# Linear attention and feed-forward on one core: the denominators of split units transposed by VectorE straight from PSUM, fewer filling products, and a new order of the steady part

## The chip, the cores and the metric

The kernel runs on one core of a Trainium2 chip. The engines that matter are TensorE (PE: matmuls; PEld: its weight loads), VectorE (DVE), ScalarE (ACT), GpSimd (POOL) and the queue that issues transfers (SP). The metric is device time in microseconds (us), the median of three runs; lower is better.

## The reference, cut to what matters

```python
# attention: 8 batches x 8 heads, 576 tokens, head size 64, 128 features
phi(x)  = exp(h - max(h)) / sqrt(128),  h = x @ omega.T - sum(x*x)/2,  x scaled by 64 ** -0.25
q_p, k_p = phi(q), phi(k)
kv  = einsum('bhsm,bhsd->bhmd', k_p, v);  z = sum(k_p, axis=2)
num = einsum('bhsm,bhmd->bhsd', q_p, kv)
den = einsum('bhsm,bhm->bhs', q_p, z)[..., None] + 1e-06
attn = num / den
# feed-forward on x = attn with the heads side by side: 4608 tokens x 512
h = x @ w_in                      # 512 x 2048
out = gelu(h) @ w_out             # 2048 x 512, gelu with erf
```

The sum of squares and the factors common to numerator and denominator cancel and aren't computed; the 1e-06 is kept, scaled.

## The kernel before, in words

**Work.** Attention is done in 32 units of two heads each (four units to a batch). The first eight units are "plain": float32 products. The other 24 are "split": a float32 value is carried as a high and a low part, and products use the parts. The feed-forward takes the tokens in 13 blocks: block 0 of 128 tokens in float32 (lines 1176 and 1202), blocks 1 to 11 of 384 tokens and block 12 of 256, whose operands are split into two float16 parts. Of such a block `mm1` (L1181) makes 16 chunks of h with 12 products each, ScalarE applies gelu (L1189) and casts the high part (`g_high`, L1193), VectorE makes the low part (`g_low`, L1197), and `mm2` (L1205 to L1207) multiplies with the second weight.

**A unit's end.** For each half of a unit's tokens (288 columns for both heads), `num_plain` (L737) or `num` (L746) writes numerators and denominators into two PSUM tiles called `pn`, out of a ring `at` of three buffers that the attention's other products use too (in the first batch, other rings too). In a plain unit `rcp` (L763 to L766) lets VectorE transpose the denominator in 32x32 blocks from PSUM into `rt`, so that nine columns hold what is different, adds the small constant, takes the reciprocal of 128x9 values, and transposes these back, spread over 32 columns. In a split unit the numerator of one head lies beside the denominator of the same head in the other half of the partitions. There `den` (L757) is two ScalarE instructions that copy the two denominators of 64x288 from PSUM into one tile `dt` and add the constant; `rcp` then transposes `dt` (L768), takes the reciprocal (L769) and transposes back (L770). Last `div` (L803 in split units) multiplies into the tokens `xs` of the feed-forward, and the two `pn` tiles come free.

**Order.** Nothing is ordered at run time: each engine runs its own list. A planner at build time simulates all operations with a cost each (the second argument of `op`), and picks on each engine the ready operation with the earliest due time. Due times come from `STARTS` (blocks), `UDUE` (halves of units) and `OFF` (an offset for each kind of operation), with bonuses from `X`. The first operations, those named in the list `FIRST`, are put in the order of that list; it holds those of the first part, up to the middle of block 1. What comes after it follows the due times: the steady part, in which the products of blocks and those of attention units are interleaved.

**Filling products.** Where the planner finds TensorE without work, and its own clock is between `wk0` and `wk` microseconds, it emits `fill` (L381): four products of 128 columns of the identity matrix, whose result, in the unused columns 384 to 511 of the first buffer `hb`, is read by nobody.

**Queues.** SP issues all transfers in one order: `load_dup` (q and k of a split unit), `load_vst` (v of a batch), the weights' pieces, and the stores of finished rows. `x_low` (L894), `k_shift` (L920), `k_high` (through the helper at L352) and `w_round` (L453) are GpSimd's.

Of the kernel before, what the change touches and what calls it, by code (L numbers as in the profile page):

```python
# [14 lines left out]
AF = mybir.ActivationFunctionType  # L15
ALU = mybir.AluOpType
# [3 lines left out]
P = 128  # L20
T = 384
# [3 lines left out]
TOP = 13  # L25
TBS = (128,) + (384,) * 11 + (256,)

X = dict(fb=793.51, fbp=-272.45, fb0=327.13, fbb=-89.81, fbw=0.0, pm=0.088, tsw=1.28, wmaxp=0, plain=8, kvp=8, eb0=8, ttr=1,
         pair=0, amax=0, qm=1, xm=0, km=0, prelu=1, vs=1, rm=1, wk=100.0, wk0=5.0, nd=1, sr=0, pmx=0, m0=5)

STARTS = (526.64, 413.1, 498.14, -519.29, 750.73, 290.96, 409.8, 1471.02, 410.3, 561.38, 1804.53, 1092.9, 2449.47, 1437.07)
UDUE = (138.05, 1052.37, 451.76, -315.56, -8.29, -412.87, -648.85, -667.31, -702.59, -616.51, 659.91, -322.47, 26.1, 555.78,
# [4 lines left out]
OFF = dict(block_be=26.55, block_high=27.77, block_low=-66.27, block_out=-28.64, block_scales=3.6, block_spread=19.77,  # L39
           bound_b=-1.8, bound_c=-2.45, chain_a=-30.63, chain_b=-10.13, chain_c=-20.24, den=42.52, div=27.82, exp_tiles=19.68,  # L40
           exps=188.48, g_high=-4.72, g_low=-2.69, gelu=-0.61, k_high=-188.65, k_low=1.15, k_shift=6.34, kv=-46.75, kv_a=19.82,
           kv_b=26.2, kv_b2=28.0, kv_c=85.59, kv_d=-177.32, kv_split=-133.22, kvz_plain=-8.08, load_dup=-16.98, load_om=49.87,
           load_two=-48.56, load_v=-10.04, load_vraw=0.87, load_vst=9.94, mm1=-0.7, mm2=6.86, nothing=115.9, num=-9.4,
           num_plain=-14.95, p2=-1.38, pair=14.61, proj=20.5, proj_add=90.32, proj_lo=-1.05, proj_q=-2.91, q_back=-44.1,
           q_blocks=93.79, q_copy=3.3, q_high=-144.85, q_low=-2.94, q_max=87.36, q_max2=100.29, q_max3=-0.43, q_max4=12.08,
           q_max5=4.81, q_max6=-30.09, q_shift=-0.46, q_trans=-45.18, rcp=31.74, shared=-0.95, shift_tiles=7.84,
           split_om=35.99, store=-8.53, store_dma=-54.03, top=-1.35, v_a=53.83, v_b=-6.0, v_max=-0.96, v_scales=80.74,
           w_hi=58.87, w_high=6.68, w_lo=0.74, w_load=-11.85, w_low=3.77, w_rmax=11.16, w_round=-18.28, warm=5.19,
           wchain_a=35.94, wchain_b=91.67, wchain_c=-1.79, wchain_d=18.88, wchain_e=5.29, wchain_f=-87.86, x_high=-1.56,
           x_low=0.31, zeros=71.27)  # L50
FIRST = (1, 3, 0, 2, 6, 7, 8, 40, 4, 5, 42, 110, 76, 144, 41, 142, 10, 9, 151, 157, 44, 13, 43, 11, 14, 15, 47, 74, 16, 45, 17,
# [208 lines left out]
def favor_attention_ffn(ctx: ExitStack, tc: tile.TileContext, qT, kT, v, omT, w_in, w_out, out):  # L260
    nc = tc.nc
    B, H, D, S = qT.shape
    NJ = H // 2
# [4 lines left out]
    TB = TBS  # L268
    NBLK = len(TB)
    T0 = [sum(TB[:n]) for n in range(NBLK + 1)]  # L270
    assert T0[-1] == NTOK
    NF = F // P
    R2 = 2 * S
    NT = R2 // P
    NV = v.shape[3]
    HS = S // 2
    EPS = 1e-6 * M
# [5 lines left out]
    N32 = 1  # L283
# [12 lines left out]
    w32 = cp.tile([P, 2, NF, 512], I32, name="w32")  # L296
    w32f = w32.bitcast(F32)
    wi32 = w32f[:, 1].rearrange("p c (j w) -> p c j w", j=NJ)
# [19 lines left out]
    iz = ident.bitcast(BF16)  # L318
# [4 lines left out]
    op = PL.op  # L323
# [54 lines left out]

    def fill():
        for i in range(4):  # L380
            nc.tensor.matmul(hb[0][:, T:], iz[:, 0:P], iz[:, P:], start=True, stop=True)  # L381

    def load_om():
        for r in range(2):
# [209 lines left out]
    for b in range(B):  # L594
        for j in range(NJ):
            u = Obj()
# [162 lines left out]
    def rcp(u, half):  # L759
        rt, rc = G['rt', u, half], G['rc', u, half]  # L760
        rv = rt.rearrange("p (n c) -> p n c", c=32)
        if X['nd'] and not u.split:
            nc.vector.transpose(rt, G['pn', u, half, 1][:, 0:HS])  # L763
            nc.vector.tensor_scalar(rc, rv[:, :, 0], EPS, None, op0=ALU.add)
            nc.vector.reciprocal(rc, rc)
            nc.vector.transpose(rv, rc.unsqueeze(2).broadcast_to([P, HS // 32, 32]))  # L766
            return
        nc.vector.transpose(rt, G['dt', u, half])  # L768
        nc.vector.reciprocal(rc, rv[:, :, 0])  # L769
        nc.vector.transpose(rv, rc.unsqueeze(2).broadcast_to([P, HS // 32, 32]))  # L770
# [8 lines left out]
    def xs_place(n, j):  # L779
        if (n, j) not in xplace:  # L780
            if n < 2:
                xplace[n, j] = (xa[:, j, T0[n]:T0[n + 1]], ('xa', n, j))
            elif n == 2:
                xplace[n, j] = (None, ('xs', n, j))
            else:
                k = NKK + xk[0] % (NF - NKK)
                xk[0] += 1
                xplace[n, j] = (w32f[:, 1, k, 0:T], ('xw', k))
        return xplace[n, j]

    def xs(n, j):
        return xplace[n, j][0] if n != 2 else G['xs', n, j]
# [27 lines left out]
    def out_ops(u, half):  # L820
        ps, keys, new, pn = finish_unit(u, half)
        qs = (half,) if X['qm'] else (half, 2 + half)
        r = [('qh', u, g) for g in ((0, 1, 2) if not u.split else qs)]
        rr = [('kvz', u), ('qh', u)] if not u.split else [('kvh', u), ('kvl', u), ('qh', u)] + [('ql', u, g) for g in qs]
        ring = ANY if u.b == 0 else 'at'
        op('PE', 1.06 if not u.split else 0.8, num if u.split else num_plain, u, half, r=r + rr, w=keys,
           new=[(ring, k) for k in pn] + new)
        n = 0.5 if not u.split else 0.96
        if X['nd'] and not u.split:
            op('DVE', 1.06, rcp, u, half, r=pn, new=[('rt', ('rt', u, half)), ('rc', ('rc', u, half))])  # L830
        else:
            op('ACT', n, den, u, half, r=pn + ([('vsc', u.b)] if not u.kp else []), new=[('dt', ('dt', u, half))])
            op('DVE', 0.92, rcp, u, half, r=[('dt', u, half)], new=[('rt', ('rt', u, half)), ('rc', ('rc', u, half))])
        c = sum(0.15 + (c1 - c0) / 960 for _, c0, c1, _ in ps) * (2 if u.split else 1)
        op('DVE', c, div, u, half, due=(2, 2 * u.k + half, 0.0, 0.0), r=pn + [('rt', u, half)], w=keys + [k for _, k in new])
# [336 lines left out]
    def mm1(n, c, p):  # L1172
# [5 lines left out]
        for i in range(p * NJ, (p + 1) * NJ):  # L1178
            j, k = divmod(i, 3)
            w = (wih, wil, wih)[k][:, j, c * P:(c + 1) * P]  # L1180
            nc.tensor.matmul(h[:, 0:t], w, (G['xh', n, j], G['xh', n, j], G['xl', n, j])[k][:, 0:t], start=(i == 0), stop=(i == 3 * NJ - 1))  # L1181

    def gelu(n, c):
        t = TB[n]
        h = G['h', n, c][:, 0:t]
        if n < N32:
            nc.scalar.activation(G['g', n, c][:, 0:t], h, AF.Gelu)
        else:
            nc.scalar.activation(h, h, AF.Gelu, scale=G['bs', n][:, 2:3])  # L1189
# [37 lines left out]
    def when(n, c, add=0.0):  # L1227
        return (1, n + int(c >= NF), c % NF / NF, add)
# [16 lines left out]
    def ffn_first(n, c):  # L1245
        t = TB[n]
        k = 'F' if n >= N32 else 'F0'
        if n < N32:
            xr = [xs_place(n, j)[1] for j in range(NJ)]
            for p in range(3):  # L1250
                seq('m1', 'PE', (t * 4 / 2400 + .005) * (2, 1, 1)[p], mm1, n, c, p, r=[('w32', 1, c)] + xr, w=[('h', n, c)] if p else [],
                   new=[] if p else [('h', ('h', n, c))], due=when(n, c + p / 3), kind='P')
            op('ACT', 0.1 + t / 1000, gelu, n, c, r=[('h', n, c)], new=[('g', ('g', n, c))], tab='g', kind=k)
            return
        for p in range(3):
            xr = [(x, n, j) for j in sorted({i // 3 for i in range(p * NJ, (p + 1) * NJ)}) for x in ('xh', 'xl')]
            seq('m1', 'PE', 4 * (t / 2400 + .0025), mm1, n, c, p, r=[('wh', 1, c), ('w', 1, c)] + xr, w=[('h', n, c)] if p else [],
               new=[] if p else [('h', ('h', n, c))], due=when(n, c + p / 3), kind='P')
        op('ACT', 0.165 + t / 1000, gelu, n, c, r=[('bs', n)], w=[('h', n, c)], tab='g', kind=k)
        op('ACT', 0.15 + t / 900, g_high, n, c, r=[('bs', n), ('h', n, c)], new=[('gh', ('gh', n, c))], kind=k)  # L1260
        op('DVE', 0.09 + t / 850, g_low, n, c, r=[('bs', n), ('h', n, c), ('gh', n, c)], new=[('gl', ('gl', n, c))], kind=k)
# [135 lines left out]
```

## Time and profile before

| what | value |
|---|---|
| median of three runs | 976.9 us (976.35 to 977.07) |
| the profiled execution's own time | 975.53 us |
| its span in the trace | 973.8 us |
| PE busy | 963.4 us (99% of the span) |
| DVE, ACT, POOL busy | 715.4, 730.0, 350.4 us |
| granted TensorE clock | full speed |

Busy PE is counted from the start of a product to its modelled end; products overlap, so a product's mean duration in the tables (say 326 ns) is longer than the time from one start to the next. The pieces of the chain of work that ended last are free of that overlap. The span is the trace's; the time is the run's own clock around it, 1.7 us more here, and the profiled run lies 1.4 us below the median of the three.

### The profile page before, as it was taken

The numbers are of one execution on the slowest core, as the hardware profiler recorded it, in microseconds if no ns is written. First come the engines' busy times: TensorE is split into PE (matmuls) and PEld (weight loads), VectorE is DVE, ScalarE is ACT, GpSimd is POOL, SyncE is SP. The second block draws the span as 40 slices with busy tenths as digits, with TensorE's granted clock in tenths as the row PEclk, the third lists the DMA queues.
The fourth block names the chain that finished last, engine by engine and source line by source line (L and its number), as shares of the span: only waits on it lengthen the run. The fifth ranks groups of instructions, "written<-read, shape, count | busy, mean of one in ns | idle before, by whom it ended". The sixth has DMA issues, their size and how long they took to land.

```text
span 973.8 us, 18152 instructions
## 1 busy us (share of the span) xinstructions
PE 963.4 (99%) x6324; PEld 602.3 (62%) x6324; DVE 715.4 (73%) x1948; ACT 730.0 (75%) x1504; POOL 350.4 (36%) x560
## 2 busy tenths in 40 slices
PE   8999999999999999999999999999999999999998
PEld 7777665665566666666565665566656656555576
DVE  5899899977888889878797888777767778621111
ACT  6979897887689879787798878877776986643243
POOL 2444334742166264353255335245216522200000
PEclk9999999999999999999999999999999999999999
DMA  8756123321041041031221132022003200000000
GB/s 305 229 182 227 70 73 134 98 82 55 1 118 61 26 139 47 25 91 45 75 82 49 30 127 66 14 72 61 24 33 86 62 23 12 1 33 1 1 34 22
DMA packets 39083, 70.96 MB, mean 73 GB/s; under 512 B 5712, under 2 KB 14288, under 8 KB 38992
## 3 DMA queue, kind: packets, MB, share of 16 engines
q1 hardware_dynamic: 38992, 69.81, 23.1%
q8 instruction: 50, 0.82, 0.4%
q14 instruction: 41, 0.34, 0.1%
HBM read 60.36 MB, written 9.44 MB: 72 GB/s over the span
## 4 chain that ended last, share of the span: by engine, by line
PE 96%; DVE 2%; DMA 1%; ACT 0%; issue 0%; SPq 0%; ACTq 0%; DVEq 0%
PE hb L1181 37%; PE acc L1205 12%; PE acc L1207 12%; PE acc L1206 12%; PE at L746 4%; PE at L924 3%; PE at L902 3%; PE at L1003 2%; PE hb L381 2%; PE hb L1176 2%; PE acc L1202 1%; PE at L657 1%; PE at L737 1%; PE at L689 1%; PE hb L689 1%; PE at L727 1%
## 5 line engine op out<-in xcount | busy, mean ns | idle before, releaser
L1181 PE MATMUL hb<-xh,wih 128*128 128x384 f16 (+1 forms) x768 | 247.2, 322 | 0.6 <-DVE gl L1197 0.4
L1181 PE MATMUL hb<-xl,wih 128*128 128x384 f16 (+1 forms) x768 | 247.2, 322 | 0.0
L1181 PE MATMUL hb<-xh,wil 128*128 128x384 f16 (+1 forms) x768 | 247.1, 322 | 0.0
L894 POOL TENSOR_TENSOR r<-xt,r 64x256 fp32r<-64x256 f32 (+2 forms) x216 | 171.8, 814 | 202.7 <-ACT r L889 161.3
L1205 PE MATMUL acc<-woh,gh 128*128 128x512 f16 (+1 forms) x560 | 211.4, 377 | 0.0
L1207 PE MATMUL acc<-wol,gh 128*128 128x512 f16 (+1 forms) x560 | 210.5, 376 | 0.0
L1206 PE MATMUL acc<-woh,gl 128*128 128x512 f16 (+1 forms) x560 | 210.5, 376 | 0.0
L1197 DVE SCALAR_TENSOR_TENSOR gl<-hb,bs,gh 128x384 f16<-128x384 f32 (+1 forms) x192 | 115.2, 600 | 126.0 <-ACT gh L1193 124.2
L1181 PEld LDWEIGHTS <-wih 128*128 128x128 f16 x1536 | 147.0, 98 | 95.2 <-issue 1.7
L1189 ACT ACTIVATE hb<-hb,bs 128x384 f32<-128x384 f32 (+1 forms) x192 | 104.5, 545 | 86.8 <-PE hb L1181 84.5
L1193 ACT ACTIVATE gh<-hb,bs 128x384 f16<-128x384 f32 (+1 forms) x192 | 109.2, 569 | 51.5 <-PE acc L1207 35.5
L1181 PEld LDWEIGHTS <-wil 128*128 128x128 f16 x768 | 75.1, 98 | 50.2 <-issue 1.6
L889 ACT CAST r<-xt 128x256 fp32r<-128x256 f32 (+2 forms) x216 | 81.5, 403 | 25.8 <-PE at L902 10.5
L1207 PEld LDWEIGHTS <-gh 128*128 128x128 f16 x576 | 56.4, 98 | 64.5
L1205 PEld LDWEIGHTS <-gh 128*128 128x128 f16 x576 | 56.1, 97 | 47.4 <-issue 0.4
L1206 PEld LDWEIGHTS <-gl 128*128 128x128 f16 x576 | 56.5, 98 | 42.1
L803 DVE TENSOR_TENSOR w<-at,rt 64x128 f32<-64x128 f32 (+6 forms) x168 | 54.7, 325 | 4.3 <-DVE rt L770 0.5
L757 ACT ACTIVATE dt<-at,vsc 64x288 f32<-64x288 f32 x96 | 47.6, 495 | 5.2 <-PE at L746 3.0
L902 PE MATMUL at<-om,r 128*128 128x256 f32 x216 | 50.3, 325 | 0.2
L924 PE MATMUL at<-r,om 128*128 128x288 f32 x192 | 50.4, 351 | 0.0
L906 ACT COPY lo<-at 128x256 f32<-128x256 f32 (+1 forms) x120 | 40.4, 349 | 2.2 <-PE at L902 1.5
L963 DVE TENSOR_TENSOR ql<-qt,qh 128x576 fp32r<-128x576 f32 x48 | 37.3, 782 | 6.1 <-ACT qh L960 6.0
(218 smaller groups left out, 1690.6 us busy)
## 6 DMA issues: line engine op xcount, KB each, us to landing
xt<-in_kT SPq DMA_DIRECT2D x56, 288.0 KB, 3.8
xt<-in_qT SPq DMA_DIRECT2D x56, 288.0 KB, 3.6
out_x<-o SPq DMA_DIRECT2D x35, 256.0 KB, 2.1
raw<-in_w_in SPq DMA_DIRECT2D x16, 512.0 KB, 5.2
raw<-in_w_out SPq DMA_DIRECT2D x16, 512.0 KB, 4.6
w<-in_v SPq DMA_DIRECT2D x6, 1280.0 KB, 6.1
wol<-in_v SPq DMA_DIRECT2D x6, 320.0 KB, 5.9
vt<-in_v SPq DMA_DIRECT2D x2, 320.0 KB, 4.1
```

The costliest lines, as they stand in the source:

```text
L803: nc.vector.tensor_tensor(x[r, c0:c1], ps[r, r0:r1], rt[r, r0:r1], op=ALU.mult)
L889: nc.scalar.copy(G['r', u, x][:, 0:b - a], xf[:, a:b])
L894: nc.gpsimd.tensor_tensor(r, xf[D:, a:b], r, op=ALU.subtract)
L902: nc.tensor.matmul(o[:, t], r[:, t * P:(t + 1) * P], om, start=True, stop=True)
L924: nc.tensor.matmul(G['pp', u, NK + g][:, 0:HS], om[:, i], xr_part(u, NK + g), start=(i == 0), stop=(i == 1))
L1181: nc.tensor.matmul(h[:, 0:t], w, (G['xh', n, j], G['xh', n, j], G['xl', n, j])[k][:, 0:t], start=(i == 0), stop=(i == 3 * NJ - 1))
L1189: nc.scalar.activation(h, h, AF.Gelu, scale=G['bs', n][:, 2:3])
L1193: nc.scalar.activation(G['gh', n, c][:, 0:t], G['h', n, c][:, 0:t], AF.Copy, scale=G['bs', n][:, 3:4])
L1197: nc.vector.scalar_tensor_tensor(G['gl', n, c][:, 0:t], G['h', n, c][:, 0:t], G['bs', n][:, 3:4], G['gh', n, c][:, 0:t], op0=ALU.mult, op1 ...
L1205: nc.tensor.matmul(acc, gh[:, s], woh[:, c, c0:c1], start=(c == 0), stop=False)
L1206: nc.tensor.matmul(acc, gl[:, s], woh[:, c, c0:c1], start=False, stop=False)
L1207: nc.tensor.matmul(acc, gh[:, s], wol[:, c, c0:c1], start=False, stop=(c == NF - 1))
```

## The change

The edits that act are these; names in the text are those of the diff.

- `nd2=1`: for a split unit `den` isn't emitted. `rcp` transposes the two denominators from PSUM by two VectorE instructions of 64x288 each, adds the constant with a `tensor_scalar` on the 128x9 values (the constant is a number, or a column of `vsc`), takes the reciprocal and transposes back. The planner's cost of `rcp` becomes 1.65 on VectorE, in place of 0.96 on ScalarE and 0.92 on VectorE. An empty operation takes `den`'s place, so that the numbers in `FIRST` stay valid.
- `wk` goes from 100 to 60: `fill` is emitted only while the planner's clock is below 60.
- `fill` has `start=False` in place of `start=True`.
- `STARTS`, `UDUE`, `OFF` and the bonuses in `X` (`fb`, `fbp`, `fb0`, `fbb`, `pm`) have new values. `FIRST` is the same.
- `e0=0` guards another way to do block 0 (`hcols`, `mm1_early`), which is therefore not used.

```diff
-X = dict(fb=793.51, fbp=-272.45, fb0=327.13, fbb=-89.81, fbw=0.0, pm=0.088, ..., wk=100.0, wk0=5.0, nd=1, ...)
+X = dict(fb=697.83, fbp=-306.98, fb0=177.38, fbb=-52.98, fbw=0.0, pm=0.071, ..., wk=60.0, wk0=5.0, nd=1, ..., nd2=1, e0=0)
-STARTS = (526.64, 413.1, 498.14, -519.29, ...)
+STARTS = (516.2, 589.47, 506.17, -529.12, ...)
...
     def fill():
         for i in range(4):
-            nc.tensor.matmul(hb[0][:, T:], iz[:, 0:P], iz[:, P:], start=True, stop=True)
+            nc.tensor.matmul(hb[0][:, T:], iz[:, 0:P], iz[:, P:], start=False, stop=True, skip_group_check=True)
...
     def rcp(u, half):
...
+        if X['nd2']:
+            for r, ps in ((slice(0, D), G['pn', u, half, 0][D:P, 0:HS]), (slice(D, P), G['pn', u, half, 1][0:D, 0:HS])):
+                nc.vector.transpose(rt[r], ps)
+            nc.vector.tensor_scalar(rc, rv[:, :, 0], EPS if u.kp else G['vsc', u.b][:, 1:2], None, op0=ALU.add)
+            nc.vector.reciprocal(rc, rc)
+            nc.vector.transpose(rv, rc.unsqueeze(2).broadcast_to([P, HS // 32, 32]))
+            return
         nc.vector.transpose(rt, G['dt', u, half])
...
     def out_ops(u, half):
...
+        elif X['nd2']:
+            op(None, 0, nothing)
+            op('DVE', 1.65, rcp, u, half, r=pn + ([('vsc', u.b)] if not u.kp else []), new=[('rt', ('rt', u, half)), ('rc', ('rc', u, half))])
         else:
             op('ACT', n, den, u, half, r=pn + ([('vsc', u.b)] if not u.kp else []), new=[('dt', ('dt', u, half))])
             op('DVE', 0.92, rcp, u, half, r=[('dt', u, half)], new=[('rt', ('rt', u, half)), ('rc', ('rc', u, half))])
```

More of the change, by code (lines that the diff above doesn't have):

```diff
@@ L26 @@
 TBS = (128,) + (384,) * 11 + (256,)
[L28 to L34, printed above, removed]
[4 rows of a table removed]
@@ L39 @@
[L39 to L50, printed above, removed]
@@ new lines @@
+X = dict(fb=697.83, fbp=-306.98, fb0=177.38, fbb=-52.98, fbw=0.0, pm=0.071, tsw=1.28, wmaxp=0, plain=8, kvp=8, eb0=8, ttr=1,
+         pair=0, amax=0, qm=1, xm=0, km=0, prelu=1, vs=1, rm=1, wk=60.0, wk0=5.0, nd=1, sr=0, pmx=0, m0=5, nd2=1, e0=0)
+STARTS = (516.2, 589.47, 506.17, -529.12, 647.96, 206.28, 448.9, 1464.25, 472.07, 730.48, 2070.68, 1429.24, 2423.39, 1936.22)
+UDUE = (228.89, 1046.05, 373.58, -255.21, 66.86, -379.94, -547.54, -713.44, -754.53, -687.13, 647.32, -393.41, -159.09, 615.54,
[4 rows of a table added]
@@ new lines @@
+OFF = dict(block_high=-10.59, block_low=-54.75, block_out=-14.13, block_scales=19.54, block_spread=56.15, bound_a=-18.57,
+           bound_b=-28.86, bound_c=39.92, chain_b=22.53, chain_c=3.35, chain_d=-3.44, div=-53.04, exp_tiles=-16.96, exps=41.3,
+           g_high=22.9, g_low=56.16, gelu=77.17, identity=5.72, k_high=-67.41, k_low=26.35, k_shift=-96.2, kv=144.63,
+           kv_a=-2.67, kv_b=-10.17, kv_b2=-22.67, kv_c=-19.14, kv_d=1.23, kv_split=-82.07, kvz_plain=-37.77, load_dup=14.17,
+           load_om=9.77, load_two=-2.99, load_v=-65.34, load_vst=17.51, mm1=-12.89, mm2=0.03, nothing=4.98, num=-4.26,
+           num_plain=46.27, p2=0.89, proj=0.28, proj_add=65.54, proj_lo=0.36, proj_q=-61.22, q_back=12.91, q_blocks=64.45,
+           q_copy=14.02, q_high=-186.21, q_low=47.41, q_max=-0.62, q_max3=-4.63, q_max4=-15.46, q_max6=20.47, q_shift=-4.88,
+           q_trans=131.97, rcp=30.74, scale_om=84.98, shared=7.06, shift_tiles=25.98, store=-98.5, store_dma=-1.34, top=-42.14,
+           v_a=40.02, v_b=7.73, v_copy=82.28, v_max=3.45, v_scales=23.18, v_spread=-3.42, w_hi=-7.4, w_high=-0.29, w_lo=-0.23,
+           w_load=129.31, w_low=-23.65, w_rmax=50.21, w_round=-17.18, w_shift=-29.01, warm=34.47, wchain_b=2.77,
+           wchain_c=-9.66, wchain_d=-2.52, wchain_f=-28.66, x_high=-67.4, x_low=0.64, zeros=-0.17)
@@ L272, in favor_attention_ffn @@
     NF = F // P
+    HG = 3
     R2 = 2 * S
@@ L1181, in mm1, with hcols, mm1_early @@
             nc.tensor.matmul(h[:, 0:t], w, (G['xh', n, j], G['xh', n, j], G['xl', n, j])[k][:, 0:t], start=(i == 0), stop=(i == 3 * NJ - 1))
+    def hcols(c):
+        return G['h', 0, c // HG * HG][:, c % HG * TB[0]:(c % HG + 1) * TB[0]]
+    def mm1_early(c, j):
+        nc.tensor.matmul(hcols(c), wi32[:, c, j], xs(0, j)[:, 0:TB[0]], start=(c % HG == 0 and j == 0), stop=(j == NJ - 1), skip_group_check=True)
     def gelu(n, c):
         t = TB[n]
+        if n < N32 and X['e0']:
+            nc.scalar.activation(G['g', n, c][:, 0:t], hcols(c), AF.Gelu)
+            return
         h = G['h', n, c][:, 0:t]
@@ L1249, in ffn_first @@
             xr = [xs_place(n, j)[1] for j in range(NJ)]
+            if X['e0']:
+                if c % HG == 0:
+                    key = ('h', n, c)
+                    cs = range(c, min(c + HG, NF))
+                    for j in range(NJ):
+                        for x in cs:
+                            op('PE', t * 4 / 2400 + .02, mm1_early, x, j, r=[('w32', 1, x), xr[j]], w=[key] if (x, j) != (c, 0) else [],
+                               new=[] if (x, j) != (c, 0) else [('h', key)], due=when(n, x + j / 4), kind='P')
+                op('ACT', 0.1 + t / 1000, gelu, n, c, r=[('h', n, c // HG * HG)], new=[('g', ('g', n, c))], tab='g', kind=k)
+                return
             for p in range(3):
```

8 rows, old and new, of the table UDUE are left out of this document.

## The prediction

> **What bounds the kernel now.** I read the page first: the engines' busy time and the chain that ended last.
>
> ```profile
> PE 963.4 (99%) x6324; PEld 602.3 (62%) x6324; DVE 715.4 (73%) x1948; ACT 730.0 (75%) x1504; POOL 350.4 (36%) x560
> PE 96%; DVE 2%; DMA 1%; ACT 0%; issue 0%; SPq 0%; ACTq 0%; DVEq 0%
> ```
>
> TensorE carries the chain; ScalarE, which the change relieves, has none of it. Since an average hides stages, the windows come second (busy us in each stretch).
>
> ```profile
> 64.00:105.00 41.00, 39.98 (x332) 30.05 (x328) 37.87 (x72) 35.03 (x55) 19.30 (x20) 1.00 0.56 191
> 105.00:200.00 95.00, 94.91 (x596) 57.93 (x593) 86.59 (x233) 79.23 (x156) 42.94 (x65) 1.00 0.29 86
> 200.00:800.00 600.00, 599.76 (x3669) 362.44 (x3667) 485.44 (x1390) 489.00 (x1014) 254.16 (x427) 1.00 0.20 60
> 850.00:974.00 124.00, 119.81 (x752) 73.31 (x750) 22.11 (x41) 43.11 (x83) 0.00 (x0) 1.00 0.05 18
> 100.00:150.00 50.00, 50.00 (x339) 31.92 (x335) 45.84 (x113) 45.41 (x84) 20.46 (x27) 1.00 0.24 69
> 350.00:400.00 50.00, 50.00 (x313) 30.75 (x312) 45.38 (x135) 44.23 (x95) 20.70 (x41) 1.00 0.28 84
> ```
>
> The columns are PE, PEld, DVE, ACT, POOL, the granted clock, the transfers. From 105 on PE is never without a product. Busy isn't pace, since products overlap; so third the chain's pieces, in which a start-to-start time shows (start, us, what), and what PE waited for between 105 and 850 us.
>
> ```profile
> 340.24 3.90 PE hb L1181 x24
> 410.14 2.01 PE hb L1181 x12
> 502.46 1.46 PE hb L1181 x8
> 879.31 3.90 PE hb L1181 x24
> PE hb L1181 <- DVE gl L1197: 0.4, 1, 0.4
> ```
>
> 3.90/24 = 0.1625 us per product in mid-kernel, as in the tail at 879, where nothing competes. By that pace 12 products take 1.95 and 8 take 1.30: the piece at 410 loses 0.06, that at 502 loses 0.16. With the one idle wait of 0.4 us (at 848.65) this is the scale of what another order can win from 200 to 850: 0.6 us in these rows, and I allow 2 us for losses that stand in no row here. So 124 us of tail and 650 us of steady part are TensorE's own work, which the change leaves alone.
>
> **The change part by part.**
>
> *ScalarE's copies go.* Rows by line and form; the last number group is busy us, mean ns of one, then idle time before.
>
> ```profile
> L757 ACT ACTIVATE dt<-at,vsc 64x288 f32<-64x288 f32 x96 | 47.6, 495 | 5.2 <-PE at L746 3.0
> L768 DVE STREAM_TRANSPOSE rt<-dt 128x288 f32<-128x288 f32 x48 | 22.7, 472 | 11.6 <-ACT dt L757 11.5
> L763 DVE STREAM_TRANSPOSE rt<-at 128x288 f32<-128x288 f32 x9 | 4.3, 479 | 2.3 <-PE at L737 2.1
> L803 DVE TENSOR_TENSOR w<-at,rt 64x288 f32<-64x288 f32 x24 | 10.9, 453 | 0.8
> L800 DVE TENSOR_TENSOR xs<-at,rt 128x288 f32<-128x288 f32 x4 | 1.8, 446 | 0.0
> L764 DVE TENSOR_SCALAR rc<-rt 128x9 f32<-128x9 f32 x16 | 5.3, 329 | 0.6
> ```
>
> 96 x 0.495 = 47.6 us leave ScalarE, and VectorE's 11.5 us of waiting for `dt`. All of it lies beside full PE windows: worth 0 by itself. What is late next at those 48 places is TensorE's `num`: `rcp` now waits for it directly. A VectorE that comes early stands, with `g_low` and the divisions queued behind it; plain units do this already, and 2.1 us over 9 is what it cost them.
>
> *VectorE gets more.* One transpose of 128x288 becomes two of 64x288. No row has that form. PSUM as source costs the same as SBUF (479 against 472), and half the partitions cost the same (453 against 446 for another instruction), so each is about 0.478; bounds 0.24 (time by partitions) and 0.48. With the added `tensor_scalar` at its mean of 0.329 that is 0.478 + 0.329 = 0.81 us a half, 48 times: 38.7 us. The `tensor_scalar`'s own bounds come from these:
>
> ```profile
> 64.14 1.24 DVE L764 TENSOR_SCALAR rc<-rt 128x9 f32<-128x9 f32 x1
> 62.98 2.37 POOL L453 TENSOR_TENSOR w<-w 128x1024 int32<-128x1024 int32 x1 [3.81 <-ACT qh L731]
> L764 DVE TENSOR_SCALAR rc<-rt x16: 173/174/1237, 28.9 to 158.0; 128x9 f32<-128x9 f32 x16
> L894 POOL TENSOR_TENSOR r<-xt,r 64x256 fp32r<-64x256 f32 (+2 forms) x216 | 171.8, 814 | 202.7 <-ACT r L889 161.3
> ```
>
> Alone it takes 0.174; at 64.14 it ended at 65.38, just after GpSimd's instruction did, at 65.35. So the total lies between 48 x (0 + 0.174) = 8 us and 48 x (0.478 + 1.237) = 82 us; I keep 38.7, the means. From 200 to 800 VectorE then has 485 + 38.7 x 600/652 (the copies ran from 194 to 846) = 521 of 600 us, 87%. The row of 100 to 150 shows 45.84 of 50, 92%, with PE full. The cover is therefore there on the average: 0 us. It is thin at 350 to 400: 45.38 + 3.0 = 48.4 of 50. If the cover fails for a share x of it, that costs 38.7x.
>
> The Trainium skill speaks against this step: "SBUF — State Buffer", section "Who interferes with whom", has VectorE and GpSimd share a pair of ports under an exclusive lock, and a `tensor_scalar` in its two-port mode is blocked for GpSimd's whole instruction. The trace agrees at 64.14. By that rule each of the 48 may stand behind `x_low`, 0.8 us at the worst: 38 us, a VectorE sum of 48 x (0.478 + 0.174 + 0.81) = 70 us in place of 38.7; that is inside the bounds above.
>
> *Fewer filling products.* The chain itself runs through them:
>
> ```profile
> 68.05 0.67 PE hb L381 x12
> 68.83 0.91 PE hb L381 x16
> 69.77 0.28 ACT g L1187
> 70.09 0.38 PE hb L381 x4
> 78.96 0.89 PE hb L381 x16
> 83.78 0.22 PE hb L381 x4
> 103.12 0.22 PE hb L381 x4
> ACT g L1187 <- PE hb L381: 2.2, 1, 2.2
> ```
>
> The planner's 60 lies near 65 on the chip (it puts the product that starts at 64.78 at 59.8), so these 56 products, 14 fills, go. They are no mere padding of idle time: gelu's ACT instruction at 69.77 waited 2.2 us for a filling product (same buffer `hb`), and the next filling product waited for that gelu. Upper end: 0.67 + (70.47 - 68.83 = 1.64) + 0.89 + 0.22 + 0.22 = 3.6 us. Lower end 0: what comes behind may be late itself. These rows say how late:
>
> ```profile
> 68.53 1.27 DVE L678 TENSOR_TENSOR et<-at,nm 128x512 f32<-128x512 f32 x2
> 77.04 1.29 DVE L669 TENSOR_REDUCE nm<-at 128x4 f32<-128x512 f32 x2 [0.61 <-PE at L657]
> 80.29 2.36 POOL L453 TENSOR_TENSOR w<-w 128x1024 int32<-128x1024 int32 x1 [1.35 <-ACT xh L1166]
> 83.84 1.08 PE L1202 MATMUL acc<-w,g 128*128 128x512 f32 x2
> 114.61 1.29 DVE L669 TENSOR_REDUCE nm<-at 128x4 f32<-128x512 f32 x2 [0.85 <-PE at L657]
> 160.64 1.54 DVE L1027 TENSOR_REDUCE vmax<-w 128x1 f32<-128x640 f32 x2 [0.72 <-DMA w<-in_v]
> ```
>
> The product after the second group needs a buffer that the first of two subtractions (L678, done at 69.17) frees: it could start 1.3 us before 70.47, where the chain has it. The one at 83.84 needs weights that GpSimd finished at 82.65, 1.2 us ahead; GpSimd in turn waited for ScalarE. VectorE, almost full, moves forward only where it waited for PE: 0.61 + 0.85 = 1.5 us in these rows. So I keep 1.9 us, about half the upper end and near these two; the work that could eat it stands at 160.64, where VectorE waits for a transfer.
>
> *`start=False`* and *`e0`*: nothing is read of that result, and `e0` is off: 0.
>
> *The new order.* It moves every later operation on all five lists, but adds no PE work. Bounds: a gain of 2 us (above), a loss by the rivals. GpSimd's list: an `x_low` moved behind a `k_shift` waits 2.1 us of work:
>
> ```profile
> L920 POOL TENSOR_TENSOR et<-et,nm 128x1152 f32<-128x1152 f32 x13 | 27.5, 2113 | 2.9 <-DVE nm L912 2.1
> PE at L657 <- DMA xt<-in_kT: 2.0, 1, 2.0
> ```
>
> SP's list: a load behind a store that waits for its output is late by that wait, but PE's only wait for a transfer is the first load, so loads have room. I take -0.5 us: some of the tight `gl` places eased, by no row that I can name.
>
> *Sum*: -1.9 - 0.5 = -2.4 us on the span of 973.8, 971.4; the profiled execution's own time 975.53 would be 973.1. The median is 1.4 above that execution: 976.9 - 2.4 = 974.5.
>
> **The rivals.**
>
> *Hidden.* The fills' time is taken back before the steady part by VectorE (86.59 of 95 us busy from 105 to 200) at the transfer of 160.64, and the order brings nothing: 976.9 + 0 to -1, say 976.4. For it: VectorE's 92%. Against: it waits for PE on the way, 0.85 us at 114.61.
>
> *VectorE late (the other side).* `g_low` comes behind a longer `rcp` and a blocked `tensor_scalar`, and `mm2` and the next chunk's `mm1` wait, as at 848.65. If an eighth of 38.7 us is uncovered, +4.8 - 1.9 gives 979.8; it turns to "slower" from about (1.9 + 2.0)/38.7 = 10%. For it: the 48.4 of 50 us. Against: the 92% row with PE full, and 47.6 us off ScalarE, which casts what `g_low` waits for.
>
> *All of it.* The whole 3.6 us and the 2 us: 976.9 - 5.6 = 971.3. It needs GpSimd's weights earlier too.
>
> *The clock falls* without fills:
>
> ```profile
> L377 PE MATMUL hb<-w 128*128 128x256 bf16 x22 | 4.2, 380 | 1.1 <-DVE w L368 1.1
> ```
>
> At the start 22 products of 256 columns took 4.2 us, 0.19 each; at the pace of 0.1625 for 384 columns 256 take 0.108. A fall for as long would lose some 2 us: 976.9 - 1.9 + 2 = 977. Against it: no gap left by a fill exceeds 1.7 us.
>
> The Trainium skill ("TensorE: Matmul & The Clock Gate", "Part 1: The HAM clock gate") puts the window without work that lowers the clock at about 3.4 us; the trace has no such gap after the start, so it speaks for little chance.
>
> **How the numbers follow.** Forecast 0.50, hidden 0.25, VectorE late 0.14, all of it 0.08, clock 0.03. No change that a measurement of this kernel can tell is 0.2%, 1.95 us: 974.95 to 978.85. The forecast's own range, 973 to 975.5, lies mostly below it (0.46 of its 0.50), so faster is 0.46 + 0.08 = 0.54, same 0.04 + 0.25 + 0.03 = 0.32, slower 0.14. The range reaches from all of it, 971.0, to just short of an eighth uncovered, 979.5.
>
> **What the profile after would show.** L757 gone; two 64x288 transposes from PSUM of about 0.478 us a half and a `tensor_scalar` with a tail of long ones; VectorE near 754 us, ScalarE near 682. L381 256 times, none after about 62 us, and gelu no longer waiting for it; the first `mm1` of block 1 1.5 to 2.5 us earlier. PE full from 105 on. Wrong if the transposes take half (then VectorE is freer and the order's part may be larger), if PE shows waits for `gl` or `at` of several us from 200 to 850, or if the gain at 105 is gone by 200.

## The result, and the profile after

The changed kernel takes 985.5 us (median of 4 runs, 984.6 to 986.0); the kernel before takes 976.6 beside it (976.2 to 977.1). The ratio is 1.0092, with a 95% interval of 1.0080 to 1.0105: slower by 8.9 us, where 974.5 was forecast and 979.5 was the upper end of the range. The spans differ by the same 8.9 us (973.8 and 982.7).

The engines' busy time and the chain that ended last, from the page of the changed kernel:

```profile
PE 966.9 (98%) x6268; PEld 599.2 (61%) x6268; DVE 753.3 (77%) x2044; ACT 680.0 (69%) x1408; POOL 356.9 (36%) x560
PE 74%; DVE 15%; ACT 3%; issue 2%; DMA 2%; POOL 2%; SPq 0%; ACTq 0%; POOLq 0%; DVEq 0%
```

VectorE has 753.3 us (forecast 754), ScalarE 680.0 (forecast 682). PE still reads 98% busy, but VectorE's share of the chain went from 2% to 15%. The windows (busy us of PE, PEld, DVE, ACT, POOL; clock; transfers):

```profile
64.00:105.00 41.00, 39.35 (x278) 27.91 (x275) 38.75 (x75) 36.74 (x56) 20.71 (x20) 1.00 0.59 196
105.00:200.00 95.00, 94.97 (x602) 57.52 (x601) 87.46 (x236) 77.57 (x158) 42.52 (x65) 1.00 0.28 81
200.00:800.00 600.00, 594.00 (x3605) 356.49 (x3604) 510.20 (x1450) 434.64 (x912) 255.59 (x420) 1.00 0.21 60
350.00:400.00 50.00, 47.80 (x297) 29.27 (x296) 45.86 (x122) 34.86 (x81) 20.72 (x35) 1.00 0.18 52
```

From 105 to 200 PE makes 602 products where it made 596: the early gain has arrived. From 200 to 800 it makes 3605 where it made 3669, and from 350 to 400 it makes 297 where it made 313. The clock is 1.00 throughout (in the three other runs it was 0.997 to 1.000). The longest of PE's waits between 200 and 950 us (us in total, times, longest):

```profile
PE hb L1191 <- DVE gl L1216: 3.0, 5, 1.1
PE at L934 <- DVE w L810: 2.1, 1, 2.1
PE at L912 <- DVE w L810: 0.5, 2, 0.3
PE at L912 <- POOL r L904: 0.4, 1, 0.4
```

L1191 is `mm1` and L1216 is `g_low`, with the lines of the changed kernel; L810 is the split unit's `div`, and L912 and L934 are products of the attention that need a buffer `at`. Before, the same list held one wait of 0.4 us, for `g_low`.

A profile that says 98% hides smaller losses, because products overlap. I therefore took, for every product, the time to the start of the next one less what is usual for its form, and added these up. PE's own work is the same in both kernels, once the filling products are set aside. The loss, with the filling products counted wholly as loss, summed up to a time, us:

| up to | before | after | after less before |
|---|---|---|---|
| 50 | 20.9 | 20.2 | -0.7 |
| 200 | 46.7 | 44.4 | -2.3 |
| 400 | 49.9 | 54.1 | +4.2 |
| 600 | 54.4 | 60.9 | +6.6 |
| 900 | 58.8 | 67.7 | +8.9 |

So the change won 2.3 us before 200 and lost 11.2 between 200 and 900. How high the loss reads depends on what is taken as usual for a form; the difference between the two kernels from 200 on hardly does.

What the new `rcp` costs, by line and form:

```profile
L770 DVE STREAM_TRANSPOSE rt<-at 64x288 f32<-64x288 f32 x96 | 46.1, 481 | 8.3 <-PE at L746 5.4
L771 DVE TENSOR_SCALAR rc<-rt,vsc 128x9 f32<-128x9 f32 x48 | 14.5, 301 | 1.7
L772 DVE RECIPROCAL rc<-rc 128x9 f32<-128x9 f32 x48 | 10.4, 216 | 1.7
L773 DVE STREAM_TRANSPOSE rt<-rc 128x288 f32<-128x288 f32 x48 | 22.9, 478 | 1.6
```

The 64x288 transpose costs what the 128x288 one does (481 and 478 ns). The filling products, in the view by shape, and the first `mm1` of block 1:

```profile
L381 PE MATMUL hb<-ident x256: 216/219/230, 7.3 to 61.5; 128*128 128x128 bf16 x128
109.31 0.33 PE L1191 MATMUL hb<-xh,wih 128*128 128x384 f16 x1
```

Before, that `mm1` started at 111.91.

Where VectorE carries the chain, one can see the new `rcp` at the head of it. A stretch of the changed kernel's chain (start, us, what):

```profile
322.63 0.48 DVE rt L770
323.15 0.49 DVE rt L770
...
323.66 0.50 DVE rc L771
...
324.18 0.23 DVE rc L772
...
324.43 0.48 DVE rt L773
...
326.13 0.43 DVE w L810
...
326.59 1.36 DVE w L1002 x2
...
327.99 0.63 DVE gl L1216
328.62 0.04 issue
328.66 0.81 PE hb L1191 x4
```

VectorE works without a wait from 322.63 to 328.62 (the pieces left out are VectorE's too): the two transposes, constant, reciprocal, transpose back, an instruction of L1002 (`k_low`), `div`, two more of L1002, and then `g_low`. PE's `mm1` starts 0.04 us after `g_low` ends. Whatever is added in front of `g_low` in such a stretch delays that `mm1` by as much.

The trace of before already shows how tight this hand-over can be. The timeline around three of the tightest chunks in the steady part, and around the third chunk of block 1 for contrast:

```profile
409.37 0.61 DVE L1197 SCALAR_TENSOR_TENSOR gl<-hb,bs,gh 128x384 f16<-128x384 f32 x1
410.03 0.32 PE L1181 MATMUL hb<-xh,wih 128*128 128x384 f16 x1
...
501.79 0.62 DVE L1197 SCALAR_TENSOR_TENSOR gl<-hb,bs,gh 128x384 f16<-128x384 f32 x1
502.46 0.32 PE L1181 MATMUL hb<-xh,wih 128*128 128x384 f16 x1
...
620.76 0.62 DVE L1197 SCALAR_TENSOR_TENSOR gl<-hb,bs,gh 128x384 f16<-128x384 f32 x1
621.43 0.32 PE L1181 MATMUL hb<-xh,wih 128*128 128x384 f16 x1
...
117.95 0.61 DVE L1197 SCALAR_TENSOR_TENSOR gl<-hb,bs,gh 128x384 f16<-128x384 f32 x1
121.89 0.34 PE L1181 MATMUL hb<-xh,wih 128*128 128x384 f16 x1
```

At these three `g_low` ends at 409.98, 502.41 and 621.38, and `mm1`, which needs the buffer `hb` that `g_low` frees, starts 0.05 us later each time. In the stage with VectorE at 92%, on which the forecast rested, `g_low` ends at 118.56 and the `mm1` that takes its buffer starts at 121.89: 3.3 us of slack, which is long even there.

There are two buffers `hb`, so the first `mm1` of each chunk can be set against the `g_low` of the chunk but one before it. The slack between the two (estimates from the timelines' starts and ends):

| kernel, stretch in us | chunks | least, median us | under 0.06 us | under 0.8 us |
|---|---|---|---|---|
| before, 100 to 150 | 5 | 1.01, 1.74 | 0 | 0 |
| before, 200 to 850 | 139 | 0.05, 0.87 | 7 | 64 |
| changed, 200 to 850 | 136 | 0.05, 1.14 | 12 | 56 |

So 0.05 us is the least, not the rule; but the new `rcp` adds some 0.8 us to VectorE at a place, and nearly half the chunks of the steady part had less than that, where the stage of the forecast had none. Of the seven under 0.06 us one shows as a wait (0.4 us, at 848.65); the others don't.

### The profile page after: what moved, and what is told of

It is laid out like the page before. It is cut to its first block, busy times and chain, and to the rows that moved or that the text cites. A ratio compares the mean times of both kernels' runs of the same rounds, so it can differ in the third digit from the quotient of the medians.

```text
span 982.7 us, 18013 instructions
## 1 busy us (share of the span) xinstructions
PE 966.9 (98%) x6268; PEld 599.2 (61%) x6268; DVE 753.3 (77%) x2044; ACT 680.0 (69%) x1408; POOL 356.9 (36%) x560
## 4 chain that ended last, share of the span: by engine, by line
PE 74%; DVE 15%; ACT 3%; issue 2%; DMA 2%; POOL 2%; SPq 0%; ACTq 0%; POOLq 0%; DVEq 0%
PE hb L1191 29%; PE acc L1224 9%; PE acc L1226 9%; PE acc L1225 9%; PE at L746 2%; PE at L912 2%; PE at L934 2%; DVE rt L770 2%; PE at L1013 2%; DVE gl L1216 2%; DVE w L810 2%; PE hb L381 2%; POOL r L904 1%; PE at L657 1%; PE acc L1221 1%
## 5 line engine op out<-in xcount | busy, mean ns | idle before, releaser
L1191 PE MATMUL hb<-xh,wih 128*128 128x384 f16 (+1 forms) x768 | 247.2, 322 | 3.3 <-DVE gl L1216 3.0
L1191 PE MATMUL hb<-xl,wih 128*128 128x384 f16 (+1 forms) x768 | 247.3, 322 | 0.0
L1191 PE MATMUL hb<-xh,wil 128*128 128x384 f16 (+1 forms) x768 | 247.1, 322 | 0.0
L1216 DVE SCALAR_TENSOR_TENSOR gl<-hb,bs,gh 128x384 f16<-128x384 f32 (+1 forms) x192 | 114.8, 599 | 130.7 <-ACT gh L1212 129.0
L1191 PEld LDWEIGHTS <-wih 128*128 128x128 f16 x1536 | 146.9, 98 | 97.5 <-issue 1.7
L1191 PEld LDWEIGHTS <-wil 128*128 128x128 f16 x768 | 75.1, 98 | 55.0 <-issue 5.7
L810 DVE TENSOR_TENSOR w<-at,rt 64x128 f32<-64x128 f32 (+6 forms) x168 | 54.4, 324 | 2.6
L934 PE MATMUL at<-r,om 128*128 128x288 f32 x192 | 50.6, 353 | 2.2 <-DVE w L810 2.1
L770 DVE STREAM_TRANSPOSE rt<-at 64x288 f32<-64x288 f32 x96 | 46.1, 481 | 8.3 <-PE at L746 5.4
L912 PE MATMUL at<-om,r 128*128 128x256 f32 x216 | 50.2, 324 | 1.3 <-DVE w L810 0.5
L1013 PE MATMUL at<-vb,w 128*128 128x129 f16 (+3 forms) x432 | 41.1, 212 | 0.4 <-DVE w L1002 0.3
```

Of the source, the lines that this page charges most:

```text
L810: nc.vector.tensor_tensor(x[r, c0:c1], ps[r, r0:r1], rt[r, r0:r1], op=ALU.mult)
L912: nc.tensor.matmul(o[:, t], r[:, t * P:(t + 1) * P], om, start=True, stop=True)
L934: nc.tensor.matmul(G['pp', u, NK + g][:, 0:HS], om[:, i], xr_part(u, NK + g), start=(i == 0), stop=(i == 1))
L1216: nc.vector.scalar_tensor_tensor(G['gl', n, c][:, 0:t], G['h', n, c][:, 0:t], G['bs', n][:, 3:4], G['gh', n, c][:, 0:t], op0=ALU.mult, op1 ...
```

## The experiments

Two theories stood at first: VectorE's added time is what delays PE ("VectorE"), and the new order of the lists is ("order"). Kernels that share a table below ran beside the same runs of the kernel before. "Old lists" are those of the kernel before, with its line of operations on every engine unchanged; "new lists" are those of the changed kernel.

**Filling products alone** (kernel before, the last 14 of 78 fills left out of its lists):

```diff
-        put_fn(fill)
+        fills[0] += 1
+        if fills[0] <= 64:
+            put_fn(fill)
```

> The kernel before with its lists unchanged on every engine, except that the last 14 of its 78 fills (56 products) are left out. Both theories of the loss say the same here, because the fills are another part: 974 to 975 us, 2 to 2.5 us below before (976.6), with the loss up to 150 us near 42.8 us, as the changed kernel shows, where before has 45.3. If the gain of the first 150 us is not the fills' but comes from the new due times, this is 976.6, no change.

**New `rcp` in the old lists** (the edit of `rcp` alone; `den` is left out, and nothing is planned anew):

```diff
     def den(u, half):
+        if u.split:
+            return
...
     def rcp(u, half):
+        if u.split:
+            ... (the lines of nd2, as in the change above)
+            return
```

> The kernel before with every engine's list as it was, and only the instructions swapped: the 96 ScalarE copies are left out, and each rcp of a split unit has two 64x288 transposes, the tensor_scalar, the reciprocal and the transpose back. Theory 'VectorE's end' (the longer rcp on a VectorE that releases most of PE's products is what costs): at least 6 us slower than before, 983 us or more, with PE waiting for gl. Theory 'order' (the new due times make a list that is late by itself): within 2 us of before, 975 to 979.

**Old `rcp` in the new lists** (`den`'s two copies stand on ScalarE where its list has reached when `rcp` is emitted):

```diff
-        if X['nd2']:
+        if X['nd2'] and not u.split:
...
+        alloc('dt', ('dt', u, half))
+        den(u, half)
         nc.vector.transpose(rt, G['dt', u, half])
```

> The changed kernel with every engine's list as it is, and the instructions swapped back: two ScalarE copies into dt are put in ScalarE's list where rcp was planned, and rcp is the old one. Theory 'VectorE's end': VectorE is freed of 38 us, and most of the 11 us lost from 200 to 900 comes back: 975 to 978. Theory 'order': the waits stay: 983 to 988.

**New `rcp`, planned with the old due times** (the changed kernel with the old `STARTS`, `UDUE`, `OFF` and bonuses; `wk` stays 60):

> The planner plans the new rcp (cost 1.65, no copies) and stops its fills at 60, as in the changed kernel, but STARTS, UDUE, OFF and the bonuses are those of before. Theory 'VectorE's end': as slow as the changed kernel, 983 to 988, since any list carries the same 38 us. Theory 'order': the old due times give a list as good as before's, 974 to 977 with the fills' 2 us.

| kernel | us (before: 977.2) | ratio, 95% | DVE busy |
|---|---|---|---|
| late fills left out | 975.9 | 0.9985 (0.9976 to 0.9994) | |
| new `rcp`, old lists | 994.9 | 1.0178 (1.0163 to 1.0193) | 757.4 |
| old `rcp`, new lists | 1013.0 | 1.0368 (1.0337 to 1.0399) | |
| new `rcp`, old due times | 1006.6 | 1.0304 (1.0288 to 1.0320) | |

The fills are worth 1.5 us by the ratio (0.6 to 2.3), less than the 2 to 2.5 expected, and that kernel is a little faster than both. The new `rcp` alone costs 17.7 us in the old lists, twice what the whole change costs. So the new order gives back rather than takes, and "order" as the cause falls. PE's longest waits there, 200 to 900 us, and its window:

```profile
PE hb L1190 <- DVE gl L1206: 5.9, 10, 2.0
PE at L933 <- DVE w L812: 2.0, 3, 1.0
PE at L911 <- DVE w L812: 1.3, 1, 1.3
...
200.00:800.00 600.00, 588.91 (x3563) 352.10 (x3563) 506.37 (x1428) 433.96 (x903) 249.03 (x417) 1.00 0.21 60
```

The same kinds of wait as in the changed kernel, for `g_low` and `div`, only more of them; and 21 of its 134 chunks from 200 to 850 start within 0.06 us of the `g_low` that they need, where before has 7 of 139. What it loses over before is heaviest in 350 to 400 and in 500 to 600 (some 2.4 to 3.5 us per 50 us, with VectorE busy for 42 to 46 of 50) and 0.5 us or less from 650 to 800, where VectorE has about 40 of 50. Fullness alone doesn't set it: 300 to 350 has 45.1 of 50 and loses some 1.4.

The third and fourth kernel met neither expectation. In the third the trace shows why it is no clean test: ScalarE's copies come late at their new place, and VectorE stands for them (us in total, times, longest):

```profile
DVE rt L777 <- ACT dt L757: 72.7, 46, 4.1
PE hb L1193 <- DVE gl L1218: 13.6, 14, 2.5
```

What both show is that lists and instructions belong together: the old copies put into lists made without them cost 36 us, and due times found for the old costs but used with the new ones 29 us (with the new `rcp`'s time in it).

**More VectorE work, the direct wait left as it was.** The new `rcp` does two things: it adds VectorE time, and it waits for `num` directly. This kernel is the one before with ScalarE's copies in their place and, in each half of a split unit, a further transpose (overwritten by the next) and a `tensor_scalar` by 1.0.

```diff
+        nc.vector.transpose(rt[0:D], G['dt', u, half][0:D])
         nc.vector.transpose(rt, G['dt', u, half])
         nc.vector.reciprocal(rc, rv[:, :, 0])
+        nc.vector.tensor_scalar(rc, rc, 1.0, None, op0=ALU.mult)
```

> The kernel before, lists and ScalarE's copies as they are; each split rcp gets two instructions whose results change nothing: one more transpose of 64x288 and one tensor_scalar on 128x9, some 38 us of VectorE's time, and no wait of another kind. Theory 'VectorE's time' (its sheer time, in a list that hands PE its products with little to spare): 988 to 997, as in the run with the new rcp in before's lists (994.9). Theory 'direct wait' (rcp that waits for PE in place of ScalarE stands in VectorE's queue and holds up what is behind it): within 3 us of before, 975 to 980.

**The new `rcp` in the old lists without its `tensor_scalar`** (the constant isn't added to split units' denominators):

> As the run of before's lists with the new rcp (994.9), but the small constant is left out, and with it the tensor_scalar: VectorE has some 15 us less. Theory 'VectorE's time': the loss falls in proportion, from 17.7 to about 10 or 11 us, 986 to 989. Theory 'direct wait': unchanged, 993 to 996.

**A short `rcp` in the new lists, and in the old ones.** Both leave `den` out; `rcp` transposes one `pn` tile from PSUM (128x288, one instruction) and takes the reciprocal of a constant tile, so the outputs of split units are numerators over a constant. VectorE then has about as much to do as before the change.

```diff
-            for r, ps in (...):
-                nc.vector.transpose(rt[r], ps)
-            nc.vector.tensor_scalar(rc, rv[:, :, 0], EPS if u.kp else ..., None, op0=ALU.add)
-            nc.vector.reciprocal(rc, rc)
+            nc.vector.transpose(rt, G['pn', u, half, 1][:, 0:HS])
+            nc.vector.reciprocal(rc, large)
```

> The changed kernel with its lists as they are, and a split rcp as short as that of before: one transpose of 128x288 from PSUM, one reciprocal (of a constant tile), one transpose back; the constant isn't added, one of the two denominators isn't read, and the output holds numerators over a constant. VectorE has 38 us less, ScalarE's copies stay away. Theory 'VectorE's time': the 11 us of the steady part come back and the 2 us of the fills stay: 973 to 976. Theory 'order' (the new lists are late by themselves): 982 to 986.

> Before's lists without ScalarE's 96 copies, and the same short rcp (one transpose of 128x288 from PSUM, a reciprocal of a constant tile, one transpose back; the output holds numerators over a constant). VectorE's time is that of before, rcp waits for PE directly. Theory 'VectorE's time', and ScalarE's copies worth nothing: 975 to 977.5. Theory 'direct wait': 985 or more. If ScalarE's copies did hold something up, it is under 975.

| kernel | us (before: 976.3) | ratio, 95% | DVE busy |
|---|---|---|---|
| more VectorE work, old lists | 994.1 | 1.0185 (1.0169 to 1.0201) | 750.9 |
| no `tensor_scalar`, old lists | 985.7 | 1.0097 (1.0082 to 1.0112) | 744.1 |
| short `rcp`, new lists | 975.7 | 0.9995 (0.9986 to 1.0004) | 711.8 |
| short `rcp`, old lists | 974.2 | 0.9977 (0.9968 to 0.9987) | 709.9 |

The busy times of the first and of the last, and the two rows that the first adds:

```profile
PE 970.2 (98%) x6324; PEld 601.7 (61%) x6324; DVE 750.9 (76%) x2044; ACT 730.4 (74%) x1504; POOL 349.5 (35%) x560
L768 DVE STREAM_TRANSPOSE rt<-dt 64x288 f32<-64x288 f32 x48 | 22.1, 461 | 2.2 <-ACT dt L757 2.1
L771 DVE TENSOR_SCALAR rc<-rc 128x9 f32<-128x9 f32 x48 | 11.7, 243 | 1.6
```

```profile
PE 963.6 (99%) x6324; PEld 602.2 (62%) x6324; DVE 709.9 (73%) x1949; ACT 681.8 (70%) x1408; POOL 347.7 (36%) x560
200.00:800.00 600.00, 599.97 (x3674) 362.46 (x3674) 480.68 (x1391) 448.45 (x932) 252.10 (x427) 1.00 0.21 60
```

The added 35.5 us of VectorE cost 17.8 us with ScalarE's copies in their place: VectorE's time is enough as a cause, and the direct wait is not needed for it. Here 22 of 135 chunks start within 0.06 us of their `g_low`, and 4 of 140 with the short `rcp` in the old lists. Without the `tensor_scalar` VectorE is busy for 13.3 us less and the loss falls from 17.7 to 9.3 us (985.7, just under the 986 to 989 expected). The short `rcp` waits for `num` directly too and is the fastest of all that ran, 2.1 us below the kernel before in the old lists and level with it in the new. It isn't a usable version: the denominators are missing. Its 2.1 us belong to ScalarE's copies, to VectorE's wait for `dt`, and to 5.5 us less of VectorE together; these were not told apart. That it gains at all in the old lists also shows that instructions unlike those that a list was planned for need not cost anything by that alone.

**What the new lists could still have wrong.** Three kernels plan the changed kernel anew: `rcp` of split units as two operations of 0.99 and 0.96, so that `g_low` may come between; `rcp` with its measured length of 1.95 in place of 1.65; and a larger bonus `pm`.

```diff
-            op('DVE', 1.65, rcp, ...)
+            op('DVE', 0.99, rcp_t, ...)
+            op('DVE', 0.96, rcp, ...)
```

> The changed kernel, planned anew with rcp of split units as two operations of the planner (the two transposes, 0.99; the rest, 0.96), so that another operation can be put between them; the sum is the time measured, 1.95, in place of 1.65. Theory 'VectorE's time' (what it costs is the sum): 982 to 990. Theory 'long piece' (g_low stands behind one uninterrupted rcp of 2 us): 977 to 980.

> The changed kernel planned anew with rcp's cost at the measured 1.95 instead of 1.65, in one piece. Theory 'planner misled' (the lists are late because the planner counts 14 us of VectorE too little): 977 to 981. Theory 'VectorE's time': 982 to 990, and an order that was not tuned for this cost may well be worse than the changed kernel's.

> The changed kernel planned anew with the planner's margin after each operation (pm) at 0.15 us in place of 0.071, so that a product is listed later behind what releases it. Theory 'no margin' (the lists hand PE its products with nothing to spare, so each delay of VectorE is PE's): 978 to 982. Theory 'VectorE's time' with any list: 983 to 990.

**The added work behind `div`** (kernel before, old lists; a transpose and a `tensor_scalar` on a spare tile that nobody reads, after the unit has ended):

```diff
+        if u.split:
+            nc.vector.transpose(idle[0:D], rt[0:D, 0:224])
+            nc.vector.tensor_scalar(idle[:, 0:QB], idle[:, 0:QB], 1.0, None, op0=ALU.mult)
```

> The kernel before, lists and ScalarE's copies as they are; the additional VectorE work (a transpose of 64x224 and a tensor_scalar, some 34 us) comes behind the last instruction of div, so that a unit's own end and its PSUM buffers are not delayed by it, only what stands behind div in VectorE's list. If what is late is that (g_low above all): 987 to 995, as with the work inside rcp (994.1). If what is late is the unit's own end, which holds the buffers at: under 981.

| kernel | us (before: 976.8) | ratio, 95% | DVE busy |
|---|---|---|---|
| `rcp` in two, new due times | 985.2 | 1.0086 (1.0069 to 1.0103) | 752.1 |
| `rcp` at 1.95, new due times | 987.9 | 1.0118 (1.0103 to 1.0133) | |
| `pm` 0.15, new due times | 997.3 | 1.0211 (1.0196 to 1.0226) | |
| work behind `div`, old lists | 989.1 | 1.0126 (1.0111 to 1.0141) | 743.8 |

Neither the length of the piece nor the planner's wrong cost is the cause: the first is level with the changed kernel, the second slower. A larger `pm` is worse still and met neither expectation; that bonus moves the whole order, so it tells little of margins. In the last kernel the added work comes after the unit's end, and 28.4 us of VectorE still cost 12.3 us; what suffers is what stands behind in VectorE's list (19 of 136 chunks start within 0.06 us of their `g_low`). PE's longest waits there, 200 to 900 us:

```profile
PE hb L1187 <- DVE gl L1203: 5.2, 12, 1.1
PE at L908 <- DVE nm L918: 1.7, 3, 0.7
```

The price of VectorE's time, us of the kernel for each us added. Each kernel's time is first taken against the kernel before that ran beside it:

| what | kernel us | VectorE us | price |
|---|---|---|---|
| more work, old lists (against before) | 17.8 | 35.5 | 0.50 |
| work behind `div`, old lists (against before) | 12.3 | 28.4 | 0.43 |
| new against short `rcp`, old lists | 19.8 | 47.5 | 0.42 |
| no `tensor_scalar` against short `rcp`, old lists | 11.5 | 34.2 | 0.34 |
| changed kernel against short `rcp`, new lists | 9.5 | 41.5 | 0.23 |

## Why the prediction was wrong, and where it was right

**The step that failed** is "The cover is therefore there on the average: 0 us". It was read off a busy share: one stage had VectorE at 92% with PE full, and 87% was forecast elsewhere. That stage's five chunks had 1.0 us of slack or more behind `g_low`; of the steady part's 139, 64 had less than the 0.8 us that the new `rcp` adds at a place. The cover that counts is how long a product has been released before it starts, not how much of a window its releaser is idle. In place of 0, each us of VectorE time costs 0.34 to 0.50 us in the old lists, and 0.23 in the new ones, where the 41.5 us between short and new `rcp` cost 9.5. The rows for it were in the trace of before, in the timeline; the view of waits hardly shows it, because a hand-over just in time is no wait. The prediction had two of them before it: the chunks of its pieces at 410 and 502 start 0.05 us after their `g_low`, and it read of them only the 0.06 and 0.16 us lost. The sign that it named came, waits for `gl` and `at` of several us from 200 to 850.

**"VectorE late"** was the right rival, with the right mechanism (`g_low` behind a longer `rcp`, `mm2` and `mm1` waiting), and its turning point of 10% is consistent with the runs. Its size was off: it took an eighth of the time as uncovered, an assumption with no row behind it, where the new lists leave nearly a quarter uncovered and the old ones a third to a half. Its argument against itself, the 47.6 us that leave ScalarE, counted for little: all that went with them came to 2.1 us.

**"New order, -0.5"** failed as well, in both directions at once. It was asked what another order can win from the kernel before, where PE hardly waits, in place of what it must win from the kernel with the new `rcp`. There the new lists are worth 17.7 - 8.9 = 8.8 us (each against the kernel before beside it), of which the fills are 1.5. With a short `rcp` the new lists are 1.5 us worse than the old ones, even though they have the gain of the fills, so the rest of the new order is some 3 us worse there.

**"ScalarE's copies: worth 0 by itself"**: up to 2.1 us, with the reserve made above.

**The fills' step held**, in mechanism and size: 1.9 us forecast; 1.5 measured alone, 2.6 at the first `mm1` of block 1, and 2.3 by 200 us in the changed kernel. No product of L381 stands after 61.5, and the rival "Hidden" falls, since the gain at 105 is still there at 200. The clock stayed at 1.00 in the trace, so that rival falls too.

**The prices held**: 481 ns a transpose against 478; 301 ns for the `tensor_scalar` against 329; VectorE +37.9 us against +38.7; ScalarE -50.0 against -47.6.

**The port rule** of the Trainium skill ("SBUF — State Buffer", "Who interferes with whom") agrees with the trace where the two meet. VectorE's and GpSimd's instructions at one of the 48 places of the changed kernel, from its chain and its timeline:

```profile
301.55 0.57 DVE rc L771
...
299.97 2.11 POOL L930 TENSOR_TENSOR w<-w,nm 128x1152 f32<-128x1152 f32 x1
```

GpSimd's ended at 302.08, and the `tensor_scalar` at 302.12, after 0.57 us in place of 0.233, the median of the 48. Twelve of the 48 took over 0.24 us, and each of them ended some 0.03 us after an instruction of GpSimd that was running when it started. The instruction above is of 2.11 us (`k_shift`), so the prediction's worst case, 0.8 us behind `x_low`, was too low for a single place: the longest of the 48 took 0.935 us, and one in the kernel with more VectorE work 2.095. But the mean is only 301 ns, so this came to 48 x (0.301 - 0.233) = 3.3 us over the kernel and not to 38 us.

**The sum as the runs have it**: +17.7 for the new `rcp` in the old lists (ScalarE's relief is in it), -1.5 for the fills, and, as the remainder to the +8.9 measured, -7.3 by the new order.

**What stays open.** The named waits of PE add up to about 10 of the 17.7 us in the old lists; the rest is spread over late starts too small for that view, and was not split by hand-over. Why the new lists pay 0.23 and the old ones 0.34 to 0.50 was not traced to single places. The slack was followed for `mm1`'s chunks and `g_low` alone, not for the attention's products that wait for `div` and others of VectorE. Loads are a further open end. The chain of the changed kernel runs through a load of v at 339.20 that takes 5.84 us: it starts 0.06 us after VectorE's L994 (`v_b`), the last reader of the buffer, and VectorE's L1037 (`v_max`) starts some 0.03 us after it landed. So a later VectorE also makes a load late that VectorE itself needs. The three kernels with more VectorE work in the old lists have two such loads each among the longest pieces of their chains from 200 to 850, before and the short `rcp` in the old lists none; what the loads add to the time was not split off. Whether another order would hide the new `rcp` wholly was not tried.

## What to carry to other kernels

Do not take an engine's idle share for cover. Take the products of the bounding engine, look how long before its start each was released and by whom; if many have less slack behind one engine than the work that you want to add there (here 64 of 139 chunks, for 0.8 us), that engine's time is on the path, though its waits read nearly 0. Before moving work onto such an engine, add a dummy instruction of the same length there and leave the order alone: here that alone said 0.43 to 0.50 us per us. And an order worked out for certain durations belongs to them, so an edit and its order are to be judged together and also each alone.

## What was not expected of the hardware

A `tensor_scalar` on 128x9 values with a number as operand has a median of 174 ns, in the plain units of before and at the split units' places alike (the two kernels with added VectorE work); with a column of `vsc` as operand, as at all 48 places of the changed kernel, it has 233. The view by shape, of the kernel with more VectorE work and of the changed kernel (least, median and longest, ns):

```profile
L771 DVE TENSOR_SCALAR rc<-rc x48: 173/174/2095, 197.3 to 865.5; 128x9 f32<-128x9 f32 x48
```

```profile
L771 DVE TENSOR_SCALAR rc<-rt,vsc x48: 232/233/935, 195.0 to 858.7; 128x9 f32<-128x9 f32 x48
```

A transpose by blocks did not cost by its partitions: 481 ns for 64x288 against 478 for 128x288.
